# Which head VectorE takes in a shared chunk of attention scores, in a transformer-block kernel on one core

## The chip, the cores and the metric

The kernel runs on one core of a Trainium2 chip. Its engines work side by side, each with its own instruction queue in program order, and wait for one another through semaphores: TensorE (PE in the profile; PEld is its weight loads), VectorE (DVE), ScalarE (ACT), GpSimd (POOL) and SyncE (SP), which issues most of the DMAs. The metric is device time in microseconds for one execution. The median of three runs before the change is 860.53 us (859.87 to 861.01).

## The reference

One block of a transformer with adaptive layer norm: 2048 tokens of 512 features, 32 heads of 16 features, and a gated feed-forward part of width 1792.

```python
mod = (_silu(c) @ w_mod).reshape(c.shape[0], 6, 1, -1)     # sa, ca, ga, sb, cb, gb
h = _layernorm(x) * (1 + ca) + sa
q, k, v = split_heads(h @ wqkv)                            # 32 heads of 16
p = _softmax(einsum('bhqd,bhkd->bhqk', q, k) * 16 ** -0.5)
x = x + ga * (merge_heads(p @ v) @ wo)
h = _layernorm(x) * (1 + cb) + sb
x = x + gb * ((_gelu(h @ w_gate) * (h @ w_up)) @ w_down)
```

The large item is the exponential of the scores: 32 heads x 2048 x 2048 of them, which are 2048 tiles of 128 keys by 512 queries, each filling one bank of PSUM, or smaller tiles that share a bank.

## The kernel before, in words

**Units and rounds.** The queries are cut into sets of 512, 512, 512, 256, 128 and 128. A unit is one set with four heads (a "quarter" `qd` of eight); a round is a unit with one bank's worth of keys for each of its four heads. The four heads stand in the four 32-row tiles of TensorE: head position `j` of a round uses rows 32j to 32j+31. Head positions are numbered through in the list `seq`, four to a round, so the position in the list modulo 4 is the row tile.

**Chunks.** The loop in `stream` (line 1202) takes the next positions three at a time. A chunk's score matmuls (`qk`, line 1460) write three banks of `ps_sc`, one head position to a bank, and chunks alternate between two groups of three banks. ScalarE then takes the exponential of all three banks in one instruction (line 1399, 128x1536 elements) into the buffer `E`. So the scores of chunk c+2 may be written only when whoever reads chunk c has done with its banks.

**VectorE's share.** In some chunks ScalarE gets two banks (128x1024) and VectorE the third. VectorE takes the four head positions of a later round, a "quad", one bank in each of four chunks that need not follow each other. It turns scores into the bit pattern of a bf16 exponential with one multiply-add from PSUM (line 1406, `dreg<-ps_sc` or `mreg<-ps_sc`, 128x512), and after the fourth it makes four copies of the 2048 columns with the exponent bits shifted (`shift_task`, line 1484, 128x2048 each). The plain copy and the four shifted ones are multiplied with accordingly scaled values `vs`, which averages out the error of the approximation; so a quad's round costs five products with V on TensorE (`pv_mms`, line 1472, four column tiles side by side) where a plain round costs one.

**What sets the order.** All instructions are recorded by Python in an order that a planner chooses as it goes: for each engine it keeps a time of its own (`model`, line 246; `probe`, line 276), which counts for each row tile of TensorE when it is free (lines 264 to 267). At each step it picks a chunk, a product with V, a step of the projections and the feed-forward part ("side work", all through the one bank `ps_mi`, planned in `plan`, line 1128), or a filler matmul that keeps TensorE busy. A chunk gets a bank for VectorE only when the planner's time for VectorE is less than 700 ns ahead (line 1370), and there are other conditions on overdue shifts, on the three buffers for quads and on the list of candidates. So a change in how long a chunk takes in the planner's model changes what is placed afterwards, and how many quads there are.

**End of a unit.** `unit_end` (line 1506) copies the accumulator from PSUM (`osb`), sends the row of denominators through DRAM and back by a chain of DMAs on SyncE's queue (`scr_den`, `den`, `scr_rec`, four `rb`), and VectorE multiplies by the returned reciprocals (`onorm<-osb,rb`). The output projection, the layer norm and the feed-forward part of the query set follow as side work.

**The tail.** After the last exponential (`tail`, line 1548) ScalarE loads the table of gelu, and what is left of the last two sets of 128 queries is done: `wo_last` and `tail_rest` may already put their matmuls between the last chunks, since the banks of `ps_sc` come free.

Of the kernel before, what the change touches and what calls it, by code (L numbers as in the profile page):

```python
# [42 lines left out]
NS = 4  # L43
# [21 lines left out]
class _Op:  # L65
    __slots__ = ("eng", "stream", "seq", "fn", "inc", "waits", "clock", "tag", "t1")

    def __init__(self, eng, stream, seq, fn):
        self.eng = eng
        self.stream = stream  # L70
        self.seq = seq
        self.fn = fn
        self.inc = False
        self.waits = {}
        self.clock = None
        self.tag = None


class _Recorder:
# [89 lines left out]
    def rec(self, eng, fn, reads=(), writes=(), dma=None, cost=0.0):  # L169

        if self.dry:
            return None
        stream = eng if dma is None else "d_" + dma
        seq = self.count.get(stream, 0) + 1
        needs = {}

# [37 lines left out]
        if self.probing is not None:  # L214
            self.probing = max(self.probing, at)
            return None
        self.count[stream] = seq
        op = _Op(eng, stream, seq, fn)
        self.bystream.setdefault(stream, []).append(op)
        ck = self.clock[eng]  # L220
# [198 lines left out]
class _Kernel(_Recorder):  # L419
# [782 lines left out]
    def stream(self):  # L1202
# [10 lines left out]
        seq = []  # L1213
# [16 lines left out]
        for u in units[2:]:  # L1230
            n, kpb = NKT * u[3] // 512, 512 // u[3]
            plain = list(range(T0 // kpb))
            m = len(plain) * 2 // 3
# [24 lines left out]
        quad = None  # L1258

        def take(n):  # L1260
            r, i = [], pos
            while len(r) < n and i < nseq:
                if i not in vec:
                    r.append(i)
                i += 1
            return r, i
# [76 lines left out]
        while cg <= group[units[-1]]:  # L1343
            parts = early or late
            if parts and pos >= loaded and (pos >= ends[2] + 8 if early else ("ffn", 2) in self.have):
                parts.pop(0)()
                loaded = pos + (8 if early else 2)
                if not late:
                    self.done("weights")
            t = max(self.pe_now(), virt)  # L1350
            self.background(t)

            tq = None
            mem, after = take(CH - 1 if pos < nsplit + 12 and c % 2 else CH)
            s0 = CH * (c % 2)
            if mem:
                e0 = 0 if e + len(mem) > NSL else e
                if all(owner.get(e0 + i, -1) < rp for i in range(len(mem))):
                    tq = self.probe(lambda: self.mm(self.scp[:, s0:s0 + CH, 0:P], *filler))
            if tq is not None and tq <= t + 30:  # L1360
                slack = self.free["act"] - 600 - t
                w = self.next_side()
                if w is not None and pos >= w[1] and self.credit > 1536 and slack > 213 and self.probe(w[4][1]) <= t:
                    self.advance()
                    continue
                if slack > 213 and self.short(t) > 0:
                    self.mm(self.scp[:, s0, :], *filler)
                    continue
                g = None
                if len(mem) == CH and "modB" in self.have and self.free["dve"] < t + 700:  # L1370
                    while quad is None and cand and last[rounds[cand[0]][0]] < pos + AHEAD[rounds[cand[0]][0][3] == 512]:
                        cand.pop(0)
                    overdue = {x[1][1] for x in self.tasks if x[1] is not None and x[1][0] == "shift" and self.plain[x[1][1]] <= LATE}
                    if quad is not None:
                        if not overdue - {quad["rnd"][0]}:
                            g = quad["rnd"][2] + quad["j"]
                    elif (not overdue and cand and self.quad_free and (pos < ends[2] or self.credit < CREDIT or (self.next_side() is None and self.waiting[0] in ("onorm", "osb"))) and rounds[cand[0]][2] < pos + 96 and self.backlog() < BACK
                          and ("vs", rounds[cand[0]][0][1] // 2) in self.have
                          and all(k in self.have for k in self.keys(seq[rounds[cand[0]][2]]))):
                        rnd = rounds[cand.pop(0)]  # L1380
                        quad = {"rnd": rnd, "j": 0, "k": self.quad_free.pop(0), "ready": [], "n": NS + 1, "slots": {}}
                        left[rnd[0]] += NS
                        self.plain[rnd[0]] -= 1
                        g = rnd[2]
                        vec.update(range(g, g + 4))
                        mem, after = take(CH)
                if g is not None:
                    mem, after = take(CH - 1)
                items = [(m, s0 + i) for i, m in enumerate(mem)]
                if g is not None:  # L1390
                    items.append((g, s0 + len(mem)))
                self.require(sorted({k for m, _ in items for k in self.keys(seq[m])}))
                self.qk([(seq[m], k) for m, k in items])
                if c < 2:
                    (self.prologue_rest, self.prologue_v)[c]()
                n = len(mem)
                while self.step("act", self.free["act"]):
                    pass
                self.act(self.E[:, e0:e0 + n, :], self.scp[:, s0:s0 + n, :], ACT.Exp, scale=EXP_SCALE)
                for i, m in enumerate(mem):  # L1400
                    owner[e0 + i] = rof[m]
                    self.slot[m] = self.E[:, e0 + i, :]
                if g is not None:
                    j = quad["j"]
                    kq = self.kq[quad["k"]]
                    self.ts("dve", kq[:, 512 * j:512 * j + 512].bitcast(U16), self.scp[:, s0 + n, :], 128 / OCT, SHIFT_C,
                            ALU.mult, ALU.add)
                    quad["j"] = j + 1
                    if j == 3:
                        quad["ready"].append((0, [kq[:, 512 * x:512 * x + 512] for x in range(4)]))  # L1410
                        wait.append(quad)
                        for i in range(NS):
                            self.shift_task(quad, i)
                        quad = None
                if self.work and pos >= self.work[0][1]:
                    w = self.work[0]
                    rate = w[3] / max(1, w[2] - pos)
                    self.credit = min(self.credit + rate * len(items), 4096)
                pos, e, c = after, e0 + n, c + 1
                if pos >= nseq and "last" not in self.have:  # L1420
                    self.spare = [self.scp[:, x, :] for x in [*range(CH - s0, SC - s0), *range(s0, s0 + CH)]]
                    self.done("last")
                continue
            gap = 1e9 if tq is None else tq - t
            tp = pv_next()
            ok = [x[0] <= t + 30 for x in tp[:2]] + [False, False]
            w = self.next_side()
            ts = None
            side = False
            if w is not None and pos >= w[1]:  # L1430
                ts = self.probe(w[4][1])
                n = w[4][0]
                side = (ts <= t + 30 and (self.credit >= n / 2 or "last" in self.have or (self.short(t) > 0 and self.credit > -2048))
                        and n / 2.4 <= gap + max(0, self.free["act"] - 600 - t - max(0, gap)))
            if ok[0] and (ok[1] or self.pe_mode == 2 or tq is None or not mem) and not (
                    side and self.credit > 1536 and (tq is not None or not mem or self.free["act"] > t + 1200)):
                pv_do(tp[0])
                continue
            if side:
                self.advance()  # L1440
                continue
            if ok[0] and gap > 400:
                pv_do(tp[0])
                continue
            if self.short(t) > 0 and not self.open and gap > 213 and self.probe(
                    lambda: self.mm(self.mi[:, :], *filler)) <= t + 30:
                self.mm(self.mi[:, :], *filler)
                continue
            nxt = [x for x in [tq, ts] + [x[0] for x in tp] if x is not None and x > t + 30]
            if self.tasks:  # L1450
                nxt.append(max(self.free["dve"], t + 100))
            virt = min(nxt) if nxt else t + 100
# [303 lines left out]
```

## Time and profile before

| what | value |
|---|---|
| median of three runs | 860.53 us |
| the profiled execution's own time | 860.08 us |
| its span (first to last instruction) | 858.3 us |
| ScalarE busy | 831.8 us, 97% |
| TensorE busy | 797.3 us, 93% |
| VectorE busy | 700.3 us, 82% |
| exponentials by ScalarE, three banks | 372 |
| exponentials by ScalarE, two banks | 320 |
| banks taken by VectorE | 292 (73 quads) |
| granted TensorE clock, mean | 1.00 |

A share of busy time is an average over the whole span. The mean duration of an instruction in the profile counts its way through the pipeline, in which the next one has already begun; what an instruction costs a full engine is the distance from its start to the next start. A matmul on a quarter of the array overlaps with its three neighbours, and four of them are listed with their common time.

### The profile page before, as it was taken

Reading aid. Unit: us, or ns where it says so; the run is one execution under the profiler, and the core shown is the slowest. Engines: PE = TensorE matmul, PEld = TensorE weight load, DVE = VectorE, ACT = ScalarE, POOL = GpSimd, SP = SyncE. Lnnn points to the kernel's source line nnn. Section 1 sums busy time; section 2 is a strip of 40 time slices with the busy share of each in tenths; the row PEclk is TensorE's granted clock in tenths of the full one; section 3 lists DMA queues with packets and bytes.
Section 4 is the critical chain, followed back from the end, with each engine's and each line's share of the span. In section 5 each row is a group of like instructions: output and inputs, shape, how many; then the busy total and the mean of one; then the engine's idle time right before and its main releaser. Section 6 shows DMA issues by size and latency. Waiting matters only on the chain.

```text
span 858.3 us, 27911 instructions
## 1 busy us (share of the span) xinstructions
PE 797.3 (93%) x12580; PEld 288.0 (34%) x12582; DVE 700.3 (82%) x1351; ACT 831.8 (97%) x747; POOL 4.5 (1%) x12
## 2 busy tenths in 40 slices
PE   7889999999999899899999999999998999998998
PEld 3334332322222222222222222222343323345566
DVE  7865989989889989988898988989987764687575
ACT  6999999999999999999999999999999999999992
POOL 1000000000000000000000000000000000000000
PEclk9999999999999999999999999999999999999999
DMA  9000000000003111210002112120133222500000
GB/s 311 10 26 18 2 9 9 10 9 9 10 4 93 44 45 33 58 33 19 11 15 82 42 36 58 34 58 9 46 104 112 62 78 60 153 10 11 19 7 14
DMA packets 64233, 38.08 MB, mean 44 GB/s; under 512 B 17745, under 2 KB 61970, under 8 KB 64114
## 3 DMA queue, kind: packets, MB, share of 16 engines
q1 hardware_dynamic: 63056, 35.65, 14.7%
q8 instruction: 98, 1.61, 0.8%
q10 hardware_dynamic: 1058, 0.66, 0.3%
q14 instruction: 21, 0.17, 0.1%
HBM read 33.68 MB, written 2.61 MB: 42 GB/s over the span
## 4 chain that ended last, share of the span: by engine, by line
ACT 74%; PE 16%; DVE 7%; DMA 1%; issue 1%; SPq 0%; ACTq 0%; DVEq 0%
ACT E L326 72%; PE ps_mi L313 6%; PE ps_sc L313 6%; PE ps_pv L313 3%; ACT wreg L326 2%; DVE mreg L338 1%; DMA mreg<-in_w_mod_dram 1%; DVE st L366 1%; DVE wreg L343 1%; DVE hreg L338 1%; DVE wreg L347 1%; SPq L376 0%; DVE dreg L338 0%; DVE nwt L330 0%; DMA rb<-scr_rec 0%
## 5 line engine op out<-in xcount | busy, mean ns | idle before, releaser
L326 ACT ACTIVATE E<-ps_sc 128x1536 bf16<-128x1536 f32 (+2 forms) x698 | 804.1, 1339 | 11.6 <-PE ps_sc L313 11.0
L313 PE MATMUL ps_sc<-qT,kmo 32*128 32x512 bf16 (+2 forms) x1408 | 177.4, 323 | 10.1 <-ACT E L326 8.6
L313 PE MATMUL ps_sc<-qT,kme 32*128 32x512 bf16 (+2 forms) x1408 | 173.0, 323 | 12.7 <-ACT E L326 10.1
L313 PE MATMUL ps_pv<-E,vaug 128*17 128x512 bf16 (+2 forms) x2400 | 170.4, 318 | 2.4 <-DVE vaug L347 1.0
L338 DVE TENSOR_SCALAR dreg<-ps_sc 128x512 uint16<-128x512 f32 x196 | 135.1, 690 | 35.0 <-PE ps_sc L313 32.6
L338 DVE TENSOR_SCALAR mreg<-dreg 128x2048 uint16<-128x2048 uint16 x196 | 127.8, 681 | 0.4 <-PE ps_pv L313 0.4
L313 PE MATMUL ps_mi<-wreg,mreg 128*32 128x512 bf16 (+2 forms) x1504 | 110.2, 370 | 13.2 <-DVE wreg L343 6.8
L313 PE MATMUL ps_pv<-mreg,vs 128*17 128x512 bf16 (+2 forms) x1408 | 102.8, 344 | 2.1 <-DVE mreg L338 1.8
L313 PEld LDWEIGHTS ps_sc<-qT,kme 32*128 32x128 bf16 x1408 | 47.5, 91 | 130.5 <-ACT E L326 97.4
L313 PEld LDWEIGHTS ps_sc<-qT,kmo 32*128 32x128 bf16 x1408 | 47.6, 91 | 121.3 <-ACT E L326 93.6
L313 PEld LDWEIGHTS ps_pv<-E,vaug 128*17 128x17 bf16 x2400 | 53.5, 89 | 85.7 <-issue 58.2
L338 DVE TENSOR_SCALAR mreg<-ps_sc 128x512 uint16<-128x512 f32 x96 | 66.3, 691 | 16.8 <-PE ps_sc L313 15.0
L338 DVE TENSOR_SCALAR mreg<-mreg 128x2048 uint16<-128x2048 uint16 x96 | 62.9, 684 | 0.0
L313 PEld LDWEIGHTS ps_mi<-wreg,mreg 128*32 128x32 bf16 (+1 forms) x1504 | 34.1, 95 | 65.8 <-issue 20.4
L347 DVE CAST wreg<-ps_mi 128x512 bf16<-128x512 f32 x51 | 35.0, 686 | 18.2 <-PE ps_mi L313 17.7
L343 DVE SCALAR_TENSOR_TENSOR wreg<-wreg,ps_mi 128x512 bf16<-128x512 bf16 x51 | 34.9, 685 | 11.8 <-PE ps_mi L313 7.8
L313 PEld LDWEIGHTS ps_pv<-mreg,vs 128*17 128x17 bf16 x1408 | 31.6, 89 | 33.3 <-DVE mreg L338 16.8
L313 PE MATMUL ps_mi<-hreg,wreg 128*32 128x512 bf16 (+1 forms) x496 | 39.5, 377 | 1.9 <-DVE hreg L338 1.0
L313 PE MATMUL ps_mi<-wo,onorm 128*32 128x512 bf16 x480 | 37.8, 383 | 0.1
L330 DVE TENSOR_TENSOR wreg<-wreg 128x1024 bf16<-128x1024 bf16 (+1 forms) x60 | 35.9, 603 | 0.7
L330 DVE TENSOR_TENSOR onorm<-osb,rb 128x512 bf16<-128x512 f32 (+2 forms) x44 | 23.4, 536 | 11.7 <-DMA rb<-scr_rec 11.6
L313 PE MATMUL ps_mi<-mreg,hreg 128*32 128x512 bf16 x384 | 32.3, 384 | 0.0
(147 smaller groups left out, 566.0 us busy)
## 6 DMA issues: line engine op xcount, KB each, us to landing
mreg<-in_B_w_up_dram SPq DMA_DIRECT2D x25, 256.0 KB, 3.2
mreg<-in_B_w_gate_dram SPq DMA_DIRECT2D x21, 256.0 KB, 2.9
rb<-scr_rec SPq DMA_DIRECT2D x96, 32.0 KB, 1.8
mreg<-in_B_w_down_dram SPq DMA_DIRECT2D x12, 256.0 KB, 2.8
dreg<-in_B_w_down_dram SPq DMA_DIRECT2D x9, 256.0 KB, 3.0
mreg<-in_w_mod_dram SPq DMA_DIRECT2D x1, 2048.0 KB, 11.2
out_dram<-xs SPq DMA_DIRECT2D x15, 128.0 KB, 1.8
xs<-in_A_x_dram SPq DMA_DIRECT2D x3, 512.0 KB, 9.0
```

Source lines behind the costliest of these rows:

```text
L313: return self.rec("pe", lambda e: e.matmul(out, lhsT, rhs, start=start, stop=stop, tile_position=tp), [lhsT, rhs], [out], cost=(n, int(rhs ...
L326: return self.rec("act", lambda e: e.activation(out, in_, func, scale=scale, **kw), rd, wr, cost=self.cost("act", out, [in_], "act"))
L330: return self.rec(eng, lambda e: e.tensor_tensor(out, a, b, op), [a, b], [out], cost=self.cost(eng, out, [a, b], "tt"))
L338: return self.rec(eng, lambda e: e.tensor_scalar(out, a, s1, s2, **kw), rd, [out], cost=self.cost(eng, out, [a], "ts") + (60 if len(rd) > ...
L343: return self.rec("dve", lambda e: e.scalar_tensor_tensor(out, a, s, b, op0=op0, op1=op1), rd, [out], cost=self.cost("dve", out, [a, b], " ...
L347: return self.rec(eng, lambda e: e.tensor_copy(out, in_), [in_], [out], cost=self.cost(eng, out, [in_], "ts"))
L366: return self.rec("dve", lambda e: e.bn_stats(out, in_), [in_], [out], cost=self.cost("dve", out, [in_], "bn"))
```

## The change

Before, the quad's banks were taken in the order of its head positions, 0, 1, 2, 3, whatever the other two banks of the chunk held. ScalarE's two banks of such a chunk hold two following head positions of the list, for instance 0 and 1 or 2 and 3. Two score matmuls with the same head position stand in the same 32 rows of TensorE. After, the quad keeps a list of the head positions that it still needs; once the two positions of ScalarE are known (`mem`), it takes the first one on the list whose row tile is not among theirs, or the first one where all are. The buffer's column for a head position is as before, and so is what follows the fourth bank.

```diff
                     if quad is not None:
                         if not overdue - {quad["rnd"][0]}:
-                            g = quad["rnd"][2] + quad["j"]
+                            g = quad["rnd"][2]
...
-                        quad = {"rnd": rnd, "j": 0, "k": self.quad_free.pop(0), "ready": [], "n": NS + 1, "slots": {}}
+                        quad = {"rnd": rnd, "j": [0, 1, 2, 3], "k": self.quad_free.pop(0), "ready": [], "n": NS + 1, "slots": {}}
...
                 if g is not None:
                     mem, after = take(CH - 1)
+                    busy = [seq[m][2] for m in mem]
+                    j = min(quad["j"], key=lambda j: j in busy)
+                    quad["j"].remove(j)
+                    g = quad["rnd"][2] + j
                 items = [(m, s0 + i) for i, m in enumerate(mem)]
...
                 if g is not None:
-                    j = quad["j"]
                     kq = self.kq[quad["k"]]
                     self.ts("dve", kq[:, 512 * j:512 * j + 512].bitcast(U16), self.scp[:, s0 + n, :], 128 / OCT, SHIFT_C,
                             ALU.mult, ALU.add)
-                    quad["j"] = j + 1
-                    if j == 3:
+                    if not quad["j"]:
                         quad["ready"].append((0, [kq[:, 512 * x:512 * x + 512] for x in range(4)]))
```

No instruction is added or removed by these lines themselves; the order and the number of instructions change through the planner, which runs on the same code otherwise.

## The prediction, made before the changed kernel ran

> **What bounds the kernel now.** I read the busy line and the chain first, then ScalarE's groups by shape, then its waits, then one stretch of the timeline.
>
> ```profile
> PE 797.3 (93%) x12580; PEld 288.0 (34%) x12582; DVE 700.3 (82%) x1351; ACT 831.8 (97%) x747; POOL 4.5 (1%) x12
> ...
> ACT 74%; PE 16%; DVE 7%; DMA 1%; issue 1%; SPq 0%; ACTq 0%; DVEq 0%
> ```
> ```profile
> L326 ACT ACTIVATE E<-ps_sc 128x1536 bf16<-128x1536 f32 x372 | 530.7, 1540 | 1.7 <-PE ps_sc L313 1.2
> L326 ACT ACTIVATE E<-ps_sc 128x1024 bf16<-128x1024 f32 x320 | 323.8, 1120 | 1.4 <-PE ps_sc L313 1.2
> ```
> ScalarE is full: between its 692 large exponentials it sat idle 3.1 us in all. What one costs is not the 1540 or 1120 ns of these rows, in which neighbours overlap, but its step in the chain of waits, where each line is one exponential between two tanh instructions:
>
> ```profile
> 349.90 1.34 ACT E L326
> ...
> 519.55 0.92 ACT E L326
> ```
> So three banks cost 1.34 us, two 0.92, and a bank that VectorE takes over saves ScalarE 0.42 us. The kernel is 14 us of start, some 820 us of ScalarE's steps with almost no hole, and 22 us of tail.
>
> TensorE and VectorE are behind that. What the change touches is seen in the timeline of TensorE alone: a chunk whose three matmuls are in different row tiles, then one in which the third, VectorE's, has the rows of one of ScalarE's two:
>
> ```profile
> 303.42 0.39 PE L313 MATMUL ps_sc<-qT,kmo 32*128 32x512 bf16 x3
> 303.74 0.39 PE L313 MATMUL ps_pv<-E,vaug 128*17 128x512 bf16 x4
> ...
> 304.71 0.39 PE L313 MATMUL ps_sc<-qT,kmo 32*128 32x512 bf16 x2
> 304.94 0.37 PE L313 MATMUL ps_sc<-qT,kme 32*128 32x512 bf16 x1
> 305.25 0.40 PE L313 MATMUL ps_mi<-wreg,mreg 128*32 128x512 bf16 x4
> ```
> Three matmuls in three row tiles run together, and the next group starts 0.32 us after them. In the second chunk VectorE's matmul begins 0.23 us late, behind one in the same rows, and the next group starts 0.54 us after the first. A clash costs TensorE 0.22 us. It also holds up VectorE, whose waits for its banks are these (total in us, times, longest):
>
> ```profile
> DVE dreg L338 <- PE ps_sc L313: 32.6, 109, 1.2
> ...
> DVE mreg L338 <- PE ps_sc L313: 15.0, 46, 0.8
> ```
> VectorE waits 47.6 us for its scores, which is most of the slack that it has while quads are running.
>
> **The change part by part.** Counts are from the order in which the two built programs stand.
>
> *Clashes.* Before, 145 of the 292 chunks with a VectorE bank have two matmuls in one row tile; after, 29 of 304. 116 x 0.22 = 26 us less on TensorE. Not on the path: over any 24 chunks TensorE's work, priced from its rows, is below ScalarE's time already before, and ScalarE's waits bound the gain at 1.7 us (3.1 less some 1.4 us of holes in the start and at the last chunk, which stay). I take 0 and keep -1.7 for the range.
>
> *Three more quads.* The planner finds room for 12 more VectorE banks: 332 two-bank and 360 three-bank exponentials where there were 320 and 372. On ScalarE: 12 x (1.34 - 0.92) = -5.0 us. This is on the path, since ScalarE is the path.
>
> *What the quads cost.* VectorE: 12 banks and 12 shifted copies. Four copies in a row took 2.36 us in the chain, 0.59 each, and a bank's row is the same size of work (691 ns mean against 681), so 24 x 0.6 = 14.4 us. TensorE: 12 rounds with V more, 12 x 0.22 = 2.6 us, inside the 26 freed. VectorE's cover is the wait for scores: 116 clashes x 0.23 = 27 us come free of the 47.6. If that cover fails locally, a late VectorE holds its bank, the scores two chunks later wait, then ScalarE. I summed VectorE's work between successive banks against ScalarE's time: the largest backlog is 1.17 us before, 1.25 after, over 0.8 us at 6 places before and 14 after. A bank can be late by the steps of about two chunks (2 x 0.92) less its own 0.6, that is 1.2 us, before ScalarE notices. So the bound is 0 below and, if each of the 8 added places loses half of its 0.8, 3.2 us above; I take +0.3, nearest to the trace, in which 6 such places gave next to no idle time.
>
> *Side work and DMAs.* TensorE's side matmuls and SyncE's 403 issues keep their number. Only the places move: in the last stage the output projection of the fifth query set comes some 11 chunks earlier, and with it the first part of that set's feed-forward. Fillers go from 396 to 400 matmuls (nothing).
>
> *The tail.* Its head is bound by TensorE, as the chain shows:
>
> ```profile
> 836.43 0.83 PE ps_mi L313 x13
> 837.27 0.56 PE ps_pv L313 x32
> ...
> 838.15 2.40 PE ps_sc L313 x35
> ...
> 840.57 0.69 DVE hreg L343
> 841.26 0.62 DVE st L366
> ```
> The last exponential ends at 836.34, yet the last products with V start at 837.20 because 13 matmuls of the side work stand ahead, and the statistics start at 841.18, 4.84 us after it. In the changed order those 13 (and 3), two of the output projection's and 12 of 16 gate matmuls stand before the last exponential's products. Then: products at +0.15, accumulator copy 0.68 later as in the trace and 0.29 long, to +1.12; denominators, and their reciprocal from about +1.8 to +2.75 (0.95); gelu product 0.6, normalisation 0.29; last projection, and statistics at about +4.2 (all durations from the tail's rows). So -0.6 us. Bounds: 0 if this work only moves into the last chunks' holes, -1.8 (the wait of ScalarE before the first gelu, 1.82 us) if all of it goes.
>
> *Sum.* -5.0 + 0.3 - 0.6 = -5.3 us: 860.08 to 854.8 us for the profiled execution. That one lies 0.45 us below the median, so on the median's scale 855.2; I give 855.0.
>
> [...] All windows of 20 us inside the stream have a granted clock of 1.00, with TensorE at 17 to 20 us busy in nearly all. [...] The trace speaks for no throttling: start and tail are emptier (14.9 us in the first 20) and still show 0.97 to 1.00.
>
> **The rivals.**
>
> *Slower: VectorE stuck behind a DMA with a bank in its queue.* The multiply by returned reciprocals stands in VectorE's queue, and the DMAs are sometimes later than the planner thought: 11.6 us of such waits in 6 cases, the longest 4.3 us, at 798.7 to 803.0, with no bank following closely, so ScalarE lost nothing. In the changed order, three such multiplies of the last stage (chunks 617, 665 and 673 of 692) have a VectorE bank directly behind them, where the order before has two. Each can cost 4.3 - 1.2 = 3.1 us; with three, 9.3, giving 864. It decides when it passes 5.6 us, an average of 1.9 at each (7.3 for a measurable loss). Against it: the tightest (673) has 7.2 us of ScalarE time between the reciprocal (666) and its use, and such a stretch took 7.5 us in the trace (786.59 to 794.13), so I see 0.3 us late there, within the 1.2.
>
> *Same: the saving is given back.* The 14 tight places of VectorE, at 0.4 us each (half of their 0.8), lose 5.6 us, which is all of the -5.0 and -0.6: 860.5.
>
> *Larger gain.* The stream's holes go too and the tail shortens fully: -5.0 - 1.7 - 1.8 = -8.5, 852.0.
>
> *No effect of the change itself* (row tiles not the cause of the late start): speaks against it that three different tiles start together and two alike do not. Even so the 12 banks would have moved.
>
> [...]
>
> **How the numbers follow.** Forecast (853.5 to 857.2) 0.70; larger gain 0.11; partly given back (857.2 to 858.8) 0.07; same 0.05; stuck VectorE 0.06; half clock 0.01. A difference of 0.2%, 1.7 us, is about what a measurement of this kernel can tell. Faster 0.70 + 0.11 + 0.07 = 0.88, same 0.05, slower 0.07. For 8 in 10 the range goes from 852.4 (most of the larger gain) to 858.0 (half of the partly given back).
>
> **What would show it.** Right: 332 and 360 exponentials at the same steps of 0.92 and 1.34; idle before them under 3.5 us; VectorE's wait for scores down from 47.6 to about 25; three matmuls of a chunk listed as starting together; the last exponential's end near 831 and a tail of 21 to 22 us after it. Wrong: ScalarE idle "<-PE ps_sc" of more than 4 us in the stream, with VectorE waiting for `rb` just ahead; or PEclk under 9 in a slice.

## The result, and the profile after

The changed kernel takes 856.41 us, the median of six runs (854.46 to 857.85), against 860.20 us for the kernel before in six runs beside it (858.69 to 861.62). The ratio is 0.9953 (95% interval 0.9934 to 0.9972): faster by 0.47%. The forecast was 855.0 us in a range of 852.4 to 858.0. The profiled execution takes 854.46 us where that of before takes 860.08, so 5.6 us less against a forecast of 5.3; but the medians differ by only 3.8 us. That gap of almost 2 us is the part that the prediction did not see; and 0.9 of the 5.6 us is chance in the first transfers, as the table below shows.

The page of the changed kernel, its busy line and the chain's shares by engine:

```profile
PE 779.2 (91%) x12676; PEld 283.9 (33%) x12676; DVE 711.0 (83%) x1375; ACT 826.2 (97%) x747; POOL 4.5 (1%) x12
...
ACT 86%; PE 6%; DVE 5%; DMA 2%; SPq 0%; issue 0%; DVEq 0%
```

TensorE is 18 us less busy (797.3 before), VectorE 11 us more, ScalarE 6 us less. The chain now lies on ScalarE for 86% of the span where it was 74%: TensorE has mostly left it.

ScalarE's groups by shape (count, busy us, mean ns of one, then idle time before them and who ended it):

```profile
L326 ACT ACTIVATE E<-ps_sc 128x1536 bf16<-128x1536 f32 x360 | 516.1, 1554 | 3.0 <-PE ps_sc L313 2.8
L326 ACT ACTIVATE E<-ps_sc 128x1024 bf16<-128x1024 f32 x332 | 335.0, 1121 | 0.7 <-PE ps_sc L313 0.7
```

The counts are the 360 and 332 that the order gives, and idle time is 3.7 us (3.1 before). Nothing new stands in ScalarE's way in sum. The places are new, though, as the timeline shows further down.

The chain's single steps stayed as they were:

```profile
288.21 2.26 ACT E L326 x2
...
823.31 1.34 ACT E L326
```

A three-bank step takes 1.34 us, and one of each kind 2.26, which leaves 0.92 for two banks: both as before.

TensorE's timeline at the place shown of before: in the two chunks here the three scores start together, and the next group follows 0.32 us later (29 of the 304 chunks with a VectorE bank still have two scores in one row tile):

```profile
303.14 0.39 PE L313 MATMUL ps_sc<-qT,kmo 32*128 32x512 bf16 x3
303.46 0.40 PE L313 MATMUL ps_mi<-wreg,mreg 128*32 128x512 bf16 x4
303.79 0.39 PE L313 MATMUL ps_sc<-qT,kmo 32*128 32x512 bf16 x3
```

VectorE's waits for its banks (total us, times, longest):

```profile
DVE dreg L338 <- PE ps_sc L313: 22.5, 77, 1.1
...
DVE mreg L338 <- PE ps_sc L313: 14.4, 39, 3.5
```

Together 36.9 us, against 47.6: a fall by 10.7 us, and not to about 25.

To see where the 5.6 us lie, I cut the span of each profiled execution at the start of the first large exponential and at the end of the last. Inside the stream, an instruction of ScalarE that ends later after its predecessor than a full engine needs counts as late by the difference, where that is over 20 ns; a full engine needs 1.343 us for three banks, 0.917 for two, 0.935 and 0.508 for the two sizes of tanh (all from the distances in these traces).

| part of the span, us | before | changed | difference |
|---|---|---|---|
| up to the first exponential | 14.15 | 13.29 | -0.86 |
| full steps of the stream | 815.74 | 810.62 | -5.12 |
| the first exponential itself and the late steps | 6.45 | 6.62 | +0.17 |
| tail | 22.0 | 22.2 | +0.2 |
| span | 858.3 | 852.7 | -5.6 |

The start waits for the first transfers and came out between 12.8 and 15.1 us in the profiles of this study; up to 95 us the engines have the same order before and after, so its 0.9 us is chance. The change itself is the -5.12 of the full steps and two small losses. Of the line of late steps, 4.86 us before and 5.03 after are late steps, the rest is the first exponential (1.45 us) and differences of under 20 ns.

The holes in ScalarE's stream did move. Before, the two longest after the start stood at 246.5 us (0.7) and 664.9 (1.0); now they are at 152.2 (1.2) and 222.0 (0.9), both just behind the end of a unit (as 246.5 was). The timeline of all engines at the first (start, duration, engine, instruction, in brackets the idle time before it and who ended it):

```profile
149.58 0.39 PE L313 MATMUL ps_sc<-qT,kmo 32*128 32x512 bf16 x3
...
150.04 0.69 DVE L338 TENSOR_SCALAR mreg<-ps_sc 128x512 uint16<-128x512 f32 x1 [0.26 <-PE ps_sc L313]
150.13 0.39 PE L313 MATMUL ps_pv<-mreg,vs 128*17 128x512 bf16 x4
...
150.65 0.68 DVE L347 COPY osb<-ps_pv 128x512 f32<-128x512 f32 x1
...
151.39 0.39 PE L313 MATMUL ps_pv<-E,vaug 128*17 128x512 bf16 x4 [0.44 <-DVE osb L347]
...
151.71 0.61 PE L313 MATMUL ps_sc<-qT,kmo 32*128 32x512 bf16 x6
...
152.15 1.45 ACT L326 ACTIVATE E<-ps_sc 128x1536 bf16<-128x1536 f32 x1 [1.12 <-PE ps_sc L313]
```

The old unit's last product runs from 150.13 to 150.52, the copy of the accumulator follows at 150.65, and the next unit's first product with V needs the accumulator free and waits for that copy. The scores of two chunks stand behind that product in TensorE's queue, the last ones before them began at 149.58, and ScalarE waits.

VectorE's bank at 150.04 stands ahead of the copy, but it is not the cause here: the copy starts 0.14 us after the product's end, and 0.05 us is the least at any unit's end, so the bank costs at most 0.1 us (0.3 of the 0.9 us at 222.0, where it is 0.36). The end of the same unit before shows the difference:

```profile
150.07 0.39 PE L313 MATMUL ps_pv<-E,vaug 128*17 128x512 bf16 x4
...
150.31 0.68 DVE L338 TENSOR_SCALAR mreg<-ps_sc 128x512 uint16<-128x512 f32 x1
150.91 0.68 DVE L347 COPY osb<-ps_pv 128x512 f32<-128x512 f32 x1
...
151.04 0.60 PE L313 MATMUL ps_sc<-qT,kmo 32*128 32x512 bf16 x3
...
151.81 0.39 PE L313 MATMUL ps_pv<-dreg,vaug 128*17 128x512 bf16 x4
```

There the copy came 0.45 us after the last product, later than now, and ScalarE had no hole: the scores of one more chunk (151.04) stood ahead of the new unit's first product (151.81). So what the two traces show as the cause of the hole at 152.2 is the place of the scores in TensorE's queue; no run moved them.

### The profile page after: what moved, and what is told of

Read it like the earlier page. It is cut to its first block, busy times and chain, and to the rows that moved or that the text cites. A ratio compares the mean times of both kernels' runs of the same rounds, so it can differ in the third digit from the quotient of the medians.

```text
span 852.7 us, 28122 instructions
## 1 busy us (share of the span) xinstructions
PE 779.2 (91%) x12676; PEld 283.9 (33%) x12676; DVE 711.0 (83%) x1375; ACT 826.2 (97%) x747; POOL 4.5 (1%) x12
## 4 chain that ended last, share of the span: by engine, by line
ACT 86%; PE 6%; DVE 5%; DMA 2%; SPq 0%; issue 0%; DVEq 0%
ACT E L326 83%; PE ps_sc L313 3%; ACT wreg L326 3%; PE ps_mi L313 2%; PE ps_pv L313 1%; DMA mreg<-in_w_mod_dram 1%; DMA rb<-scr_rec 1%; DVE st L366 1%; DVE hreg L338 1%; SPq L376 0%; DVE dreg L338 0%; DVE vaug L347 0%; DVE nwt L330 0%; DVE wreg L330 0%; DVE kme L338 0%
## 5 line engine op out<-in xcount | busy, mean ns | idle before, releaser
L326 ACT ACTIVATE E<-ps_sc 128x1024 bf16<-128x1024 f32 (+2 forms) x698 | 799.5, 1339 | 11.0 <-PE ps_sc L313 10.8
L313 PE MATMUL ps_sc<-qT,kme 32*128 32x512 bf16 (+2 forms) x1408 | 169.9, 323 | 21.5 <-ACT E L326 18.6
L313 PE MATMUL ps_sc<-qT,kmo 32*128 32x512 bf16 (+2 forms) x1408 | 173.1, 323 | 17.6 <-ACT E L326 16.1
L313 PE MATMUL ps_pv<-E,vaug 128*17 128x512 bf16 (+2 forms) x2388 | 172.4, 318 | 4.5 <-DVE osb L347 1.6
L338 DVE TENSOR_SCALAR dreg<-ps_sc 128x512 uint16<-128x512 f32 x204 | 140.3, 689 | 25.7 <-PE ps_sc L313 22.5
L338 DVE TENSOR_SCALAR mreg<-dreg 128x2048 uint16<-128x2048 uint16 x204 | 134.3, 683 | 1.1 <-PE ps_pv L313 1.1
L313 PE MATMUL ps_pv<-mreg,vs 128*17 128x512 bf16 (+2 forms) x1456 | 107.0, 345 | 1.9 <-DVE mreg L338 1.5
L338 DVE TENSOR_SCALAR mreg<-ps_sc 128x512 uint16<-128x512 f32 x100 | 68.8, 689 | 15.5 <-PE ps_sc L313 14.4
L338 DVE TENSOR_SCALAR mreg<-mreg 128x2048 uint16<-128x2048 uint16 x100 | 65.9, 683 | 1.8 <-PE ps_pv L313 1.7
L326 ACT ACTIVATE wreg<-wreg 128x1024 bf16<-128x1024 bf16 (+1 forms) x30 | 31.3, 1044 | 0.0
```

What stands on the lines that cost most here:

```text
L313: return self.rec("pe", lambda e: e.matmul(out, lhsT, rhs, start=start, stop=stop, tile_position=tp), [lhsT, rhs], [out], cost=(n, int(rhs ...
L326: return self.rec("act", lambda e: e.activation(out, in_, func, scale=scale, **kw), rd, wr, cost=self.cost("act", out, [in_], "act"))
L338: return self.rec(eng, lambda e: e.tensor_scalar(out, a, s1, s2, **kw), rd, [out], cost=self.cost(eng, out, [a], "ts") + (60 if len(rd) > ...
```

## The experiments

"Late steps" and "tail" below are as in the table. The ratios are against the kernel before, run beside it on the same chip.

### The changed kernel again

No edit.

> The changed kernel once more, unaltered, to see how its executions spread: two of the six so far took 854.5 us at a mean granted TensorE clock of 1.00, four took 856.4 to 857.9 at 0.994 or 0.995. Theory A (the spread is the clock): the executions fall into the same two groups, and each one's time goes with its clock, about 2 us for 0.005. Theory B (chance that has nothing to do with the clock): times and clock vary independently of each other.

Nine runs give 857.09 us (854.16 to 859.03) against 859.85: 0.9960 (0.9947 to 0.9974). The stream repeats (late steps 4.81 us, tail 22.2, the holes at the same places), so they belong to the order. The runs fall into two groups by granted clock: those at 0.999 or above take 854.2 and 854.3 us, the others, at 0.992 to 0.998, 856.5 to 859.0. Within the second group the time does not go with the clock, though theory A said that it would: two runs at 0.998 take 857.1 and 857.6 us, two at 0.994 and 0.996 only 856.5.

### Free row tiles alone

The planner counts with the old row tile, so every engine has the order of before; only the head position that VectorE takes is the new one.

```diff
-                [lhsT, rhs], [out], cost=(n, int(rhs.ap[0][1]), tp))
+                [lhsT, rhs], [out], cost=(n, int(rhs.ap[0][1]), mtp or tp))
...
+                        mtp=None if k != gk else (32 * gj, 0))
```

> The free row tile is chosen as in the changed kernel, but the planner's model is told the old row tile, so that the order on every engine and the 292 banks of VectorE are those of the kernel before; only the clashes are gone on the chip. Theory A (ScalarE's 12 fewer banks are the gain): within 2 us of the kernel before, 858.5 to 860.5; VectorE's wait for scores falls from 47.6 to about 25 us, TensorE is busy some 20 us less, and ScalarE's sum of steps stays. Rival (the clashes themselves were in the way of ScalarE): 855 to 857, as far as the changed kernel gets.

859.11 us over 12 runs, ratio 0.9989 (0.9979 to 0.9999), with late steps of 4.79 us (4.86 before) and a tail of 22.0. VectorE's waits for its banks in this kernel:

```profile
DVE dreg L338 <- PE ps_sc L313: 30.7, 99, 1.4
```

That is 32.6 before, and with the second group (15.7) 46.4 instead of 47.6. TensorE is busy 781.3 us instead of 797.3. So without the new order the freed row tiles are worth 0.7 us by the medians, which the interval only just tells from nothing. The expectation of a wait of about 25 us was wrong: 119 clashes are gone (26 are left of 145), and VectorE still waits nearly as long for its scores. Its work is as much as before (698.9 us busy, 700.3 before) in a span as long as before (857.8 us, 858.3 before), so its idle time in sum cannot fall; it only comes to the next wait sooner.

### The new order alone

The reverse: the planner counts as if the free row tile were taken, and the chip gets the positions 0, 1, 2, 3 as before, with their clashes. Every engine has the changed kernel's order.

```diff
+                    jm = min(quad["jm"], key=lambda j: j in busy)
+                    quad["jm"].remove(jm)
+                    j = quad["j"].pop(0)
...
+                self.qk([(seq[m], k) for m, k in items], *((s0 + len(mem), jm) if g is not None else ()))
```

> The converse: the order of the changed kernel on every engine, with its 304 banks of VectorE, but on the chip the head positions are taken 0, 1, 2, 3 as before, so the clashes stay. Theory A: ScalarE's steps are those of the changed kernel, 5 us less than before, and some of it is lost in holes, since TensorE is 24 us busier than the order was planned for: 855.5 to 858.5. Rival (the gain needs the free tiles on the chip): 859 to 862, with 4 us or more of new holes of ScalarE waiting for scores.

866.06 us (865.03 to 872.31), ratio 1.0084 (1.0056 to 1.0113): slower than either theory allowed. ScalarE's groups of this kernel:

```profile
L326 ACT ACTIVATE E<-ps_sc 128x1536 bf16<-128x1536 f32 x360 | 509.9, 1515 | 6.3 <-PE ps_sc L313 5.6
L326 ACT ACTIVATE E<-ps_sc 128x1024 bf16<-128x1024 f32 x332 | 332.0, 1073 | 2.7 <-PE ps_sc L313 1.6
```

The counts are the changed kernel's, so the 12 banks are saved here too. But the idle time rises from 3.7 to 9.0 us and the late steps from 5.0 us at 19 places to 16.4 at 86 (some 2 us of it in a stretch at a lower clock near 810 us: PEclk is 8 in the page's slice from 798.7 to 820.3). VectorE waits 48.3 us for its banks. So the clashes (147 in this kernel) that cost next to nothing in the order of before cost some 9 us in this one. The likely reason is that it gives TensorE and VectorE more to do between two exponentials, and with 0.22 us more per clash the scores come late. Neither half brings the gain: in runs side by side the halves alone are -0.7 and +6.2 us, both together -2.8.

### More filler matmuls

Four of the first six runs had a granted clock of 0.994 or 0.995, and TensorE is 18 us less busy than before; my guess was that the one comes from the other. `FILL` sets how much work the planner wants TensorE to have in a stretch before it adds filler matmuls; 4600 gives 580 of them instead of 400.

```diff
-FILL = 4200
+FILL = 4600
```

> The changed kernel with the planner's threshold for filler matmuls at 4600 columns instead of 4200: 580 fillers instead of 400, and by the planner's choice 308 banks of VectorE instead of 304. If the slower executions of the changed kernel come from TensorE falling idle and being throttled, all executions here are at a clock of 1.00 and at 853 to 855.5 us. If the clock does not depend on that, they spread as the changed kernel's do, 854 to 857.5.

852.59 us (849.75 to 857.04), ratio 0.9912 (0.9884 to 0.9940), faster than the changed kernel. The expectation that the spread would go is wrong: three runs at full clock take 849.8 to 850.6, three at 0.995 to 0.996 take 854.6 to 857.0. And the gain has another source: the planner counts fillers as time, places four more of VectorE's banks (356 and 336 exponentials) and keeps TensorE closer to ScalarE; late steps fall to 3.9 us and the tail to 21.5. Of the 3.8 us between its profiled execution and the changed kernel's, full steps are 1.7, late steps 1.1 and the tail 0.7. Several things moved at once, so this run does not price any of them alone.

### Two more profiles of the changed kernel

No edit; the aim was a profile of an execution at a lower clock.

> The changed kernel unaltered, for a profile of one of its slower executions: by theory A a stretch of 5 to 10 us at half clock between 790 and 815 us, preceded by some 3 us in which TensorE had less than 3000 columns of work, and new idle time of ScalarE behind it of 2 to 3 us; rival: the stretch lies elsewhere, for instance in the first 300 us. If the execution is one of the faster ones, it says nothing on this.

> A second profile of the changed kernel unaltered, with the same two readings: by theory A a stretch at half clock between 790 and 815 us and ScalarE idle behind it for 2 to 3 us; rival: elsewhere.

Both show one: 859.21 us at a mean clock of 0.992, and 855.48 at 0.995. In the second, the granted clock is 0.52 and 0.63 in the two windows of 4 us from 798 on, and 1.00 again behind them; worked out from these two at half clock, that is a stretch of 6.8 us from about 798.1 on. In the first it is 0.63, 0.50 and 0.59 in the three windows from 798 to 810 us, by the same sum 10.2 us from about 799.1 on; these are 5.1 us of clock, and its mean of 0.992 over 857.5 us leaves some 1.7 us more elsewhere. The windows at that place, first of the changed kernel's profile at full clock, then of the second of these (columns: window, its length, busy us of PE, PEld, DVE, ACT, POOL with their instructions, granted clock, DMA share, GB/s):

```profile
794.00:798.00 4.00, 2.78 (x114) 1.72 (x110) 2.71 (x5) 4.00 (x4) 0.00 (x0) 1.00 0.17 45
798.00:802.00 4.00, 3.17 (x94) 1.77 (x86) 3.65 (x8) 4.00 (x5) 0.00 (x0) 1.00 0.03 3
```
```profile
794.00:798.00 4.00, 2.78 (x120) 1.71 (x108) 3.04 (x7) 4.00 (x5) 0.00 (x0) 1.00 0.16 42
798.00:802.00 4.00, 4.00 (x66) 2.10 (x62) 2.82 (x5) 3.30 (x4) 0.00 (x0) 0.52 0.06 10
802.00:806.00 4.00, 3.95 (x93) 2.05 (x90) 2.90 (x6) 3.72 (x5) 0.00 (x0) 0.63 0.01 4
```

Up to 798 us the two are alike, TensorE busy 2.78 of 4 us in both; then one goes on at clock 1.00 and the other falls to 0.52 and 0.63, and ScalarE, full in the first, has holes:

```profile
800.66 3.44 ACT L326 ACTIVATE E<-ps_sc 128x1536 bf16<-128x1536 f32 x3 [0.70 <-PE ps_sc L313]
804.33 6.07 ACT L326 ACTIVATE E<-ps_sc 128x1536 bf16<-128x1536 f32 x5 [0.23 <-PE ps_sc L313]
```

The late steps are 8.1 and 6.4 us in the two profiles against 5.0. Between 780 and 830 us, where the stretch lies, they are 2.6 and 1.4 us against 0.1, so it costs 2.5 us (10.2 us long) and 1.3 us (6.8 us long); the first one's tail is another 1.6 us longer. Over all 17 executions of the changed kernel, four ran at 0.999 or above (854.2 to 854.5 us) and 13 below (855.5 to 859.2). Of 42 of the kernel before, 32 were at 0.999 or above (median 859.3) and ten below (860.6 to 862.1). At full clock the two differ by 4.9 us (the two profiles without their start by 4.7). The medians differ by less, and the more frequent runs at a lower clock are the shown part of it; why the two runs at 0.998 are as slow as 857.1 and 857.6 us no profile shows.

### The gate matmuls after the last products

In `tail_rest` part of the gate matmuls may stand before the last chunk's products with V. This moves them behind.

```diff
-        yield from self.until("last")
+        yield from self.until("tail")
```

> The changed kernel with one thing moved: the gate matmuls of the last 128 queries may stand in TensorE's queue only after the last products with V, not before them (48 quarter matmuls in the changed kernel, 0.84 us). Everything before the last chunk is unaltered. Theory (the predicted 0.6 us of the tail was lost because the work that moved ahead stands in front of the last products): they start 0.45 us after the last exponential's end instead of 1.11, and the tail from that end falls from 22.2 to 21.2 to 21.6 us. Rival (the tail is set by something else, VectorE's chain or ScalarE's table load): 22.0 to 22.3 as before.

855.22 us (852.22 to 856.38), ratio 0.9943 (0.9924 to 0.9961). At full clock it takes 852.2 and 852.8 us where the changed kernel takes 854.2 to 854.5, and the tail is 21.06 us instead of 22.2. The timeline of the changed kernel's tail, then of this one:

```profile
829.46 1.69 PE L313 MATMUL ps_sc<-wo,onorm 128*32 128x512 bf16 x28
830.55 1.28 ACT L326 ACT_TABLE_LOAD   x1
...
830.98 0.84 PE L313 MATMUL ps_sc<-wreg,qT 128*32 128x128 bf16 x48
831.64 0.62 PE L313 MATMUL ps_pv<-E,vaug 128*17 128x128 bf16 x32
...
835.56 0.70 DVE L366 BATCH_NORM_STATS2 st<-ps_sc 128x6 f32<-128x512 f32 x1 [0.67 <-PE ps_sc L313]
```
```profile
831.55 1.69 PE L313 MATMUL ps_sc<-wo,onorm 128*32 128x512 bf16 x28
832.63 1.28 ACT L326 ACT_TABLE_LOAD   x1
833.06 0.62 PE L313 MATMUL ps_pv<-E,vaug 128*17 128x128 bf16 x32
...
836.50 0.70 DVE L366 BATCH_NORM_STATS2 st<-ps_sc 128x6 f32<-128x512 f32 x1
```

The table load marks the end of the last exponential (830.53 and 832.61). In the changed kernel the last products start 1.11 us after it, since 28 matmuls of the output projection and 48 small ones of the gate run ahead of them; without the 48 they start 0.45 us after it, and the statistics 3.9 us after it instead of 5.0. (Behind the products the same work is recorded as 12 whole matmuls instead of 48 quarters.)

### Fillers late only

To tell the fillers' effect on the clock from their effect on the order, the order is left as it is up to 32 positions into the fifth query set, and the threshold is raised from there on: 492 fillers, and the same 360 and 332 exponentials.

```diff
-        return FILL - w
+        return (FILL if not self.late else 5400) - w
...
+            self.late = pos >= ends[3] + 32
```

> The changed kernel with more filler matmuls in the last stage alone: the planner's threshold is 5400 columns instead of 4200 once the third set of 512 and some of the set of 256 queries' chunks are past; 492 fillers instead of 400, the same 332 and 360 exponentials, the same order before that point. Theory A (the slower executions of the changed kernel come from a throttled stretch in the last stage, after TensorE had little to do there): nearly all executions at a clock of 0.999 or 1.00 and at 853.5 to 855 us. Rival (the clock falls elsewhere, or independently of the fillers): most executions stay at 0.992 to 0.998 and 856.5 to 859 us.

855.01 us (853.0 to 855.4), ratio 0.9943 (0.9930 to 0.9956). Five of six runs are at clock 1.00 and the sixth at 0.998, and nothing lies above 855.4, where beside it four of the six runs with the gate matmuls moved, without these fillers, are at 0.994 to 0.996. In this kernel's profile the windows from 790 to 810 us are all at clock 1.00. So the stretch near 798 us was, by my estimate, the source of most of the spread. The runs lie around the changed kernel's four at full clock (854.2 to 854.5); the fillers restore that time and bring nothing beyond it. This profile (late steps 6.8 us, tail 22.2) has two holes that the changed kernel's has not, 0.56 us at 656.0 and 0.65 at 685.7, but they are not the fillers' doing: TensorE's order first differs at 733.4 us. The timeline at the first of them:

```profile
654.61 1.05 PE L313 MATMUL ps_mi<-wreg,mreg 128*32 128x512 bf16 x16 [1.09 <-DMA mreg<-in_B_w_gate_dram]
...
656.03 1.45 ACT L326 ACTIVATE E<-ps_sc 128x1536 bf16<-128x1536 f32 x1 [0.45 <-PE ps_sc L313]
```

Weights came 1.09 us late to a side matmul, the scores stood behind it, and ScalarE waited 0.45 us. The changed kernel's profile has no late step over 0.2 us near there. So a late transfer can account for some of the spread that is left at full clock (853.0 to 855.4).

### The two gains together

`FILL` at 4600 with the gate matmuls moved behind, or so it was meant:

```diff
-FILL = 4200
+FILL = 4600
...
-        yield from self.until("last")
+        yield from self.until("tail")
```

> The changed kernel with the filler threshold at 4600 columns and the gate matmuls of the tail behind the last products. If the two effects add (the threshold gave 849.8 us at a clock of 1.00 and 854.6 to 857 below it, the gates 1.1 us of tail): 848.5 to 849 at a clock of 1.00, 853.5 to 856 below it, median 849 to 853. Rival: the tail of this order is already short (21.5 us against 22.2), and moving the gates brings under 0.4 us.

851.23 us (850.12 to 859.21), ratio 0.9924 (0.9896 to 0.9953): within the interval of the fillers alone. It could not be otherwise: with the threshold at 4600 no gate matmul stands ahead of the last products, so the second line of the edit moves nothing, and the program is instruction for instruction that of the kernel with 580 fillers. This is that kernel run again, and no test of whether the two gains add. The two sets of runs show how far one program spreads: the seven of twelve at 0.999 or above take 849.8 to 851.6 us, the other five 854.4 to 859.2, and the medians of six differ by 1.4 us.

And with a higher threshold for the end, now starting 40 positions before the end of the fifth query set (here too the line on the gate matmuls changes nothing in the program):

```diff
-        return FILL - w
+        return (FILL if not self.late else 5400) - w
...
+            self.late = pos >= ends[4] - 40
```

> The same with the threshold at 5400 columns in the last stage, from 40 head positions before the end of the fifth set on; 620 fillers instead of 580, the same 336 and 356 exponentials. If throttling in the last stage is what is left: the clock is 0.999 or 1.00 in nearly all executions and the median 848 to 850.5. Rival: the added fillers cost ScalarE as much as the clock did, as part of the gain was lost with 492 fillers (new holes of 0.6 us each), and the median stays at 851 or more.

851.97 us (850.81 to 853.28), ratio 0.9916 (0.9903 to 0.9929), all five runs at clock 1.00 and within 2.5 us, and faster than both the kernel before and the changed one. It is 1.5 to 4 us more than was hoped for. Its runs at full clock take 850.8 to 853.3 us, the plain 4600's 849.8 to 851.6: the extra fillers seem to cost at full clock about what they save in executions at a lower clock, and the two cannot be told apart by their medians.

## Why the prediction was right, and where it was not

**The saving on ScalarE (-5.0 us): right.** 12 three-bank exponentials became two-bank ones; the full steps of the stream fell by 5.12 us, against 12 x (1.343 - 0.917) = 5.11, and the steps themselves did not change. That the profile's 5.6 us came out so near the forecast 5.3 is in part luck: without the start's 0.9 us it is 4.7, and what is missing is in the main what the tail was to give.

**Clashes off TensorE (26 us, taken as 0): the value right, the reason incomplete.** TensorE's busy time fell by 18 us with the added products, and the clashes alone were worth 0.7 us, inside the -1.7 to 0 allowed. But I treated the 26 us as free in any order and took the saving from the 12 banks as a term of its own. The new order run with the clashes is 6 us slower than before. The terms do not stand side by side: the freed time on TensorE is the condition for the 12 banks.

**VectorE's 24 instructions (+14.4 us of work, taken as +0.3): the size right, one step wrong.** The late steps rose by 0.17 us. VectorE is 10.7 us busier. The two holes at 152 and 222 us are not of the kind that the backlog count looked for, a bank handed back late: a product that waits for the accumulator's copy stands ahead of the scores in TensorE's queue, and VectorE's bank ahead of the copy adds 0.1 and 0.3 us to them. The step that failed is the cover: VectorE's wait for scores fell to 36.9, not to about 25. I had taken 27 us out of that wait as freed and all of the added work as coming on top; with the clashes gone and nothing added, the wait fell by only 1.2 us. Earlier scores did not shorten VectorE's idle time while ScalarE's pace and VectorE's work stayed as they were; it waited further on.

**The tail (-0.6 us, between 0 and -1.8): wrong in sign.** It is 0.2 us longer. The prediction took the side work moved ahead of the last products as done in the last chunks' holes. The timeline shows it between the last exponential's scores and those products, which start 1.11 us after the last exponential's end (0.86 before) and not 0.15. With 48 of those matmuls moved behind them, the tail falls by 1.1 us. The wait before the first gelu did shrink, 1.82 to 0.59 us, but it is not on the path.

**From the profiled execution to the median (+0.45 us): wrong.** I took the offset between profile and median as the same after the change. The changed kernel's profile lies 1.95 us below its median, because that execution was one of the four in 17 at full clock. This is the largest error: the gain at full clock is 4.9 us, the medians differ by 3.8 (2.8 in the second set of runs). The last step, from 855.2 to 855.0, had no reason given.

**Half clock for a stretch (0.01): dismissed too lightly.** No run stands behind the 0.01; in the runs, 13 of 17 executions of the changed kernel had a mean clock below 0.999. The argument was that start and tail are emptier and show no loss. And the sign that the prediction named for it was there, a PEclk under 9 in a slice: at 800 us it is 8 in the page of the second profile at lower clock, and the first one's windows from 798 to 810 us stand at 0.50 to 0.63. The stretch at 794 to 798 us was the place to look at. TensorE waits there twice for ScalarE (0.61 us at 796.63, 0.52 at 797.55, in the changed kernel's profile at full clock); it is busy 2.78 of these 4 us in that profile, 2.99 and 2.78 in the two at lower clock; before, the emptiest of the six windows of 4 us from 790 to 814 us holds 3.42. In the two the clock is 1.00 up to 798 us and falls behind it.

The busy time alone does not decide it, though: the profile at full clock has the same 2.78 us and stays at 1.00, and before, TensorE was busy only 2.44 of the 4 us from 659.7 on, at a clock of 1.00. What lets the clock fall in one execution and not in another no run shows.

The stretches behind 798 us last 6.8 and 10.2 us, and the two executions are 1.0 and 4.8 us longer than the profile at full clock.

**The other rivals.** No bank was stuck behind a late DMA: the longest of VectorE's waits for returned reciprocals is 5.44 us at 719.77, with no bank behind it. Another multiply and a matmul of TensorE stood behind it, and ScalarE came 0.2 us late at 722.5. The saving was not given back at tight places (+0.17 us of late steps). The larger gain did not come from this order; with more fillers the time was as low, 851 to 853 us, for other reasons.

What is argued and not shown: that the buffer `E` was full at 152 us, so that scores could not be moved ahead; by which of its changes the order with more fillers has fewer late steps; and, for the new order with the clashes, by which waits its scores come late. None was tried by itself.

## What to carry to other kernels

Where a planner makes the order, price a change as a whole order and not as a sum: the same freed time on a second engine was worth 0.7 us in the old order and decided between -2.8 and +6.2 us in the new one. Slack that is shown as an engine's wait is not a store to draw from; ask where the next wait ends. When two edits are put together, see first whether the second still changes the program. And when a change takes work off TensorE, compare several executions with their granted clock, and look at what stands ahead of the places where it falls (here 2.78 and 2.99 of 4 us busy) and not at the average, because one profile at full clock does not tell the median.

## What the chip showed that was not expected

- Executions of one kernel on one core differ by their granted clock: 13 of 17 of the changed kernel have a mean below 0.999, and 10 of 42 before. In the two profiles at lower clock, windows from 798 us on show it at 0.50 to 0.63, which makes 10.2 and 6.8 us at half clock; the second profile of the kernel with 580 fillers, at a mean of 0.992, has a PEclk of 8 in the slice from 814.6 to 836.1 us, where the first, at 1.00, has 9 in all.
- TensorE was not idle ahead of it: in the 4 us before 798 us it was busy 2.99 and 2.78 us in these two profiles, and 2.78 us in the one in which the clock stayed at 1.00.
- The stretch of 6.8 us near 800 us costs the bound engine only 1.3 us, less than the 3.4 us of clock that are lost (0.48 and 0.37 of two windows of 4 us); ScalarE ran on for 1.8 us after the fall, to 799.96 us, from scores already written, before it waited.
- With 92 more filler matmuls in the last stage five of six runs were at 1.00; with 180 more, spread over the whole kernel, seven of twelve were at 0.999 or above.
